# Rearranging the five planned instruction queues of a two-layer transformer kernel by a table

## The chip, the cores and the metric

The kernel runs on one core of a Trainium2 chip. The core has five engines, each with an instruction queue of its own that is worked through in order: TensorE (PE in the profile, with its weight loads shown as PEld), VectorE (DVE), ScalarE (ACT), GpSimd (POOL) and SyncE (SP, which here issues all the DMA transfers). Engines wait for each other by semaphores. The metric is the device time of one execution in microseconds; a kernel's time is the median of its runs.

## The reference

The sequence has S = 2048 rows of D = 448 values; there are 16 heads of 28, and the MLP is 1792 wide. The same two blocks run twice, which makes two layers:

```python
def _A_ref(x, wqkv, wo):
    ...
    scores = jnp.einsum("bhqd,bhkd->bhqk", q, k) * (Dh ** -0.5)
    p = _softmax(scores, axis=-1)
    o = jnp.einsum("bhqk,bhkd->bhqd", p, v)
    return (lambda x, *d: x.transpose(*d))(o, 0, 2, 1, 3).reshape(B, S, D) @ wo

def _B_ref(x, w1, w2, w3, w4):
    h = _gelu(_layernorm(x, axis=-1) @ w1)
    ...
    hs = jnp.concatenate([g0, g1, g2, g3], axis=-1) @ w2
    x1 = x + hs
    h2 = _gelu(_layernorm(x1, axis=-1) @ w3) @ w4
    return x1 + h2

x = A_x
x = x + _A_ref(_layernorm(x, axis=-1), A_wqkv, A_wo)
x = x + _B_ref(_layernorm(x, axis=-1), B_w1, B_w2, B_w3, B_w4)
x = x + _A_ref(_layernorm(x, axis=-1), A_wqkv, A_wo)
x = x + _B_ref(_layernorm(x, axis=-1), B_w1, B_w2, B_w3, B_w4)
```

In `_B_ref`, g0 to g3 are the four column groups of h, shifted along the sequence by 1 or 2 rows forward or back. All inputs are bf16.

## The kernel before

**Attention.** Keys and queries are held transposed, one head per 32 partitions. A score matmul (line L1544) multiplies 32 rows of keys with 512 (in places 256) queries and fills one PSUM bank. PSUM has eight banks. Scores fill banks 0 to 2 together (a unit of three banks) and then banks 3 and 4 (a unit of two), by turns; the two or three score matmuls of a unit are called its burst. ACT turns each unit into exponentials with one instruction (L1783), 386 of them of 128x1536 and 395 of 128x1024, and writes bf16 into the buffer PT. PT holds 15 banks' worth, so that the exponentials of a unit write where those of six units earlier stood, and must wait until these were read. The reader is the product with the values, PV (L1800): a group of four matmuls, each on its own 32 columns of the array, which adds into bank 5. A few blocks of scores go to bank 6 or 7 instead and get their exponentials on DVE by a chain of integer and float operations (L1626, L1653, L1655, L1657, L1660, output PD).

**The rest of the work.** Layer norms (statistics on DVE and POOL), the projections for keys, queries and values, the output projection and the MLP of one part of the sequence are woven into the attention of another. Their matmuls are groups of four on PE, mostly at L949, and write banks 6 and 7; DVE, and ACT at the end, take the results out. The gelu of the MLP (L2237) runs on ACT in large pieces with a load of ACT's function table before and after each; the gelu before w2 is made from tanh (L2056), in the table that the exponentials use. Where normalised rows must be transposed, PE does it at the very start and end (L1173, copied out by DVE at L1180), and elsewhere they go to DRAM and back by two DMAs, written in the profile as `xnd<-xn` and `xT<-xnd`. 1041 groups of filler matmuls (L2283), whose results nobody reads, stand in PE's queue as well.

**The head.** The first keys need the weights (L975 and L977 load them in pieces of 128 and of 64 rows), a repacking on ACT (L1078), squares on ACT (L1090) whose column sums PE makes (L940), the transposed input, the key projection (L949 with wk_pad), then a bias and the query, and the first burst.

**What sets the order.** The kernel is written as generators (one for scores, one for exponentials, one for PV, and so on) that yield operations. A planner, class `Sched`, runs them against a cost table, ranks and due times, and writes 9450 operations into a `Plan`, each in the queue of its engine. `Plan.finalize` turns the dependencies into semaphore waits, and `emit` writes each queue out. Between planning and `finalize` a plan can be rearranged: `Plan.rearranged(moves, weave)` takes each pair (a, b) out of `moves`, unlinks operation number a from its engine's queue and links it in behind b, an operation of the same engine. Then it merges the five queues again in the order that the letters of `weave` give (t, s, v, g, d for PE, ACT, DVE, POOL, SP), working out the dependencies anew, and insists that every operation reads what it read before. The core of it:

```python
for (a, b) in moves:
    p, q = prv[a], nxt[a]
    nxt[p] = q
...
for (a, b) in moves:
    q = nxt[b]
    nxt[b], prv[a], nxt[a] = a, b, q
...
for c in weave:
    k = "tsvgd".index(c)
    h = heads[k]
    eng, fn, reads, writes, deps, dma, t_end = self.args[h]
```

In the kernel before, both tables are empty (`MOVES = ()`, `WEAVE = ()`, lines 19 and 20), and the call (`if WEAVE: P = P.rearranged(MOVES, "".join(WEAVE))`, line 2339) isn't made: the planner's order stands.

Of the kernel before, what the change touches and what calls it, by code (L numbers as in the profile page):

```python
# [15 lines left out]
ENGS = ("pe", "act", "dve", "pool", "sp")  # L16


MOVES = ()
WEAVE = ()  # L20

FILL_MORE = ()

# [690 lines left out]
def build_kernel(nc, A_x, A_wqkv, A_wo, B_x, B_w1, B_w2, B_w3, B_w4, out, n_layers=2):  # L714
# [85 lines left out]
    with st:  # L800
# [1531 lines left out]
        def again(fn, k):  # L2332
            return lambda e: [x for _ in range(k) for x in fn(e)]

        for (i, k) in FILL_MORE:
            args = P.args[i]
            assert args[0] == "pe" and args[2] == [("ident",)]
            P.args[i] = (args[0], again(args[1], k)) + args[2:]
        if WEAVE:
            P = P.rearranged(MOVES, "".join(WEAVE))  # L2340
        P.finalize(nc, st)
# [55 lines left out]
```

## Time and profile before

| what | us |
|---|---|
| median of three runs | 1025.24 |
| the runs | 1026.08, 1025.24, 1024.41 |
| the profiled execution | 1024.58 |
| its span in the profile | 1022.9 |
| PE busy | 960.4 |
| ACT busy | 983.0 |
| DVE busy | 798.5 |
| POOL busy | 284.3 |
| first exponential starts | 15.89 |
| last exponential has ended by | 969.85 |

The span is what the trace covers; 1.7 us of the profiled execution's time lie around it. Busy times are sums of instruction durations in which overlaps count once. An exponential starts while the one before is still in flight, so that its duration is longer than the distance between the starts of two of them. A matmul's row with "x4" is one group on four parts of the array, which run side by side.

### The profile page before, as it was taken

The page shows a single profiled execution, that of the slowest core. Times are in us where ns is not written, and L with a number is a line of the kernel's source. Part 1 is how long each engine was busy: PE and PEld are TensorE (multiplying, and loading weights), DVE is VectorE, ACT ScalarE, POOL GpSimd, SP SyncE. Part 2 cuts the span into 40 slices and gives each one's busy share as a digit, 9 for nine tenths or more (in the row PEclk, how much of TensorE's full clock was granted, in tenths as well). Part 3 has the DMA queues.
Part 4 walks back from the last instruction along what each step waited for, and adds up shares of the span by engine and source line. Part 5 has one row for each costly group of instructions (what it writes and reads, how often), then busy time and mean ns, then how long its engine had stood idle before and what let it go on. Part 6 is the DMA issues. An engine that isn't in the chain of part 4 may idle for free.

```text
span 1022.9 us, 37404 instructions
## 1 busy us (share of the span) xinstructions
PE 960.4 (94%) x16925; PEld 399.8 (39%) x16925; DVE 798.5 (78%) x1557; ACT 983.0 (96%) x898; POOL 284.3 (28%) x453
## 2 busy tenths in 40 slices
PE   8999999999989999989999899999999999999998
PEld 3332444343322344333433334334333433344475
DVE  8778988899888858887887866788788578788751
ACT  8999999999999999999999999999999999999942
POOL 3212121520343015353453301221434120432130
PEclk9999999999999999999999999999999999999999
DMA  4443331321330014110122223522312020311000
GB/s 121 140 112 103 98 105 48 58 53 36 76 66 23 13 42 101 28 42 24 48 71 70 64 62 109 150 63 87 81 25 37 28 59 17 61 46 24 13 21 25
DMA packets 99399, 62.65 MB, mean 61 GB/s; under 512 B 68712, under 2 KB 88552, under 8 KB 99240
## 3 DMA queue, kind: packets, MB, share of 16 engines
q1 hardware_dynamic: 99240, 60.27, 23.4%
q8 instruction: 132, 2.16, 0.9%
q14 instruction: 27, 0.22, 0.1%
HBM read 28.16 MB, written 16.76 MB: 44 GB/s over the span
## 4 chain that ended last, share of the span: by engine, by line
ACT 90%; PE 7%; DVE 1%; DMA 1%; issue 0%; SPq 0%; DVEq 0%; ACTq 0%
ACT PT L1783 83%; PE ps L949 6%; ACT h2T L2237 2%; ACT fb L2056 2%; ACT L1783 1%; ACT L2237 1%; DMA xT<-xnd 1%; PE ps L1544 1%; ACT vaug L2237 1%; ACT kT L2237 1%; DMA xnd<-xn 0%; DMA PT<-in_A_wqkv_dram 0%; PE ps L1800 0%; ACT sq L1279 0%; PE ps L940 0%
## 5 line engine op out<-in xcount | busy, mean ns | idle before, releaser
L1783 ACT ACTIVATE PT<-ps 128x1024 bf16<-128x1024 f32 (+1 forms) x781 | 890.8, 1406 | 2.3 <-PE ps L1544 2.2
L1544 PE MATMUL ps<-qT,kT 32*128 32x512 bf16 (+1 forms) x2304 | 268.9, 335 | 39.3 <-ACT PT L1783 30.5
L1800 PE MATMUL ps<-PT,vaug 128*32 128x512 bf16 (+1 forms) x2432 | 200.1, 340 | 0.0
L1544 PEld LDWEIGHTS ps<-qT,kT 32*128 32x128 bf16 x2304 | 69.5, 91 | 276.3 <-ACT PT L1783 269.0
L949 PE MATMUL ps<-xT,w 128*32 128x512 bf16 (+4 forms) x2656 | 169.5, 345 | 1.4 <-DVE PD L1657 1.2
L2283 PE MATMUL ps<-ident 128*32 128x256 bf16 x4164 | 156.3, 276 | 1.5 <-POOL ident L1034 1.5
L2283 PEld LDWEIGHTS ps<-ident 128*32 128x32 bf16 x4164 | 105.2, 97 | 40.9 <-issue 21.3
L1626 DVE TENSOR_SCALAR yd<-ps 128x512 int32<-128x512 f32 x97 | 66.5, 686 | 34.2 <-PE ps L1544 33.2
L949 PEld LDWEIGHTS ps<-xT,w 128*32 128x32 bf16 (+1 forms) x2656 | 63.0, 95 | 62.7 <-issue 32.0
L1800 PEld LDWEIGHTS ps<-PT,vaug 128*32 128x32 bf16 x2432 | 62.9, 95 | 48.0 <-issue 38.0
L1655 DVE SCALAR_TENSOR_TENSOR fb<-fb,yd 128x512 f32<-128x512 f32 x97 | 69.2, 714 | 0.8
L1660 DVE SCALAR_TENSOR_TENSOR PD<-yd,PD 128x512 int16<-128x512 int16 x97 | 67.9, 700 | 1.0
L1653 DVE SCALAR_TENSOR_TENSOR fb<-yd 128x512 f32<-128x512 uint16 x97 | 67.8, 703 | 0.5
L949 PE MATMUL ps<-w,h2T 128*32 128x448 bf16 x1008 | 64.4, 355 | 0.7 <-ACT h2T L2237 0.7
L1897 POOL TENSOR_TENSOR otn<-ub,fb 128x512 bf16<-128x512 f32 (+1 forms) x23 | 26.5, 1154 | 136.8 <-DMA fb<-rscr 129.4
L2215 DVE CAST h2T<-ps 128x512 bf16<-128x512 f32 (+1 forms) x67 | 42.4, 633 | 13.4 <-PE ps L949 12.4
L1140 POOL TENSOR_SCALAR vpe<-mv 128x1 f32<-128x1 f32 (+2 forms) x21 | 8.3, 393 | 149.3 <-DVE mv L1135 149.3
L1282 POOL TENSOR_TENSOR sq<-qT 128x512 bf16<-128x512 bf16 x24 | 28.1, 1175 | 66.9 <-DVE qT L1341 65.6
L1282 POOL TENSOR_TENSOR sq<-kT 128x512 bf16<-128x512 bf16 (+2 forms) x32 | 31.6, 994 | 52.9 <-DVE kT L1296 42.8
L1544 PE MATMUL ps<-wk_pad,kT 32*128 32x512 bf16 x256 | 39.0, 384 | 7.3 <-ACT PT L1783 6.2
L1657 DVE TENSOR_SCALAR PD<-fb 128x512 bf16<-128x512 f32 x98 | 41.5, 424 | 1.0
L949 PE MATMUL ps<-xT,wq_pad 128*32 128x512 bf16 x512 | 39.3, 382 | 0.7 <-DVE vaug L1386 0.7
(195 smaller groups left out, 1243.5 us busy)
## 6 DMA issues: line engine op xcount, KB each, us to landing
uscr<-ub SPq DMA_DIRECT2D x28, 256.0 KB
ub<-uscr SPq DMA_DIRECT2D x28, 256.0 KB
fb<-rscr SPq DMA_DIRECT2D x24, 256.0 KB
xnd<-xn SPq DMA_DIRECT2D x28, 128.0 KB, 2.0
xd<-x_res SPq DMA_DIRECT2D x16, 224.0 KB, 3.1
x_res<-xd SPq DMA_DIRECT2D x16, 224.0 KB, 3.1
w<-in_B_w_dram SPq DMA_DIRECT2D x5, 448.0 KB, 8.4
obf<-in_A_x_dram SPq DMA_DIRECT2D x16, 112.0 KB, 2.1
```

The source lines that it names most:

```text
L949: r.append(e.matmul(out=out[c:c + w, :], lhsT=lhsT[:, c:c + w], rhs=rhs, start=start, stop=stop, tile_position=(0, c)))
L1282: return both("sq", 0.15 + NW * 0.0018, 0.07 + NW * 0.00104, lambda e: e.tensor_tensor(out=sq[:, si, 0:NW], in0=src, in1=src, op=ALU.mult) ...
L1544: yield op("pe", (0.005 + NW * 0.00042) / nc_, lambda e, i=i, kc=kc, j=j, g=g, qt=qt, a=a, NW=NW, bank=bank: e.matmul(out=ps[:, bank, i * ...
L1626: yield op("dve", c_ps(512), lambda e: e.tensor_scalar(out=y, in0=ps[:, bi(bank), :], scalar1=SCALE * L2E * FS, scalar2=-126.0 * FS, op0=A ...
L1653: yield op(D_[0][0], D_[0][1], lambda e: e.scalar_tensor_tensor(out=q, in0=lo, scalar=E2 / E3 * FS, in1=lo, op0=ALU.add, op1=ALU.mult), re ...
L1655: yield op(D_[1][0], D_[1][1], lambda e: e.scalar_tensor_tensor(out=q, in0=q, scalar=E1 / E3 * FS * FS, in1=lo, op0=ALU.add, op1=ALU.mult) ...
L1660: yield op(D_[3][0], D_[3][1], lambda e: e.scalar_tensor_tensor(out=pdt.bitcast(I16), in0=hi, scalar=128.0, in1=pdt.bitcast(I16), op0=ALU. ...
L1783: yield op("act", EXPC + n * w * 0.000833, lambda e, bk=bk, s0=s0, n=n, w=w: e.activation(out=PT[:, s0:s0 + n, 0:w], in_=ps[:, bk[0]:bk[0] ...
L1800: r.append(e.matmul(out=ps[32 * j:32 * j + 32, 5, 0:NW], lhsT=vaug[:, vs, 32 * (4 * g + j):32 * (4 * g + j) + 32], rhs=buf[:, s, i * NW:(i ...
L2215: ev = op("dve", c_ps(m * NW), lambda e, hr=hr, pv=pv: e.tensor_copy(out=hr, in_=pv), reads=[("ps", bi(b))], writes=hk, touch=[b])
L2237: yield op("act", c_act(len(fr_) * NW), lambda e, v=v: e.activation(out=v, in_=v, func=ACT.Gelu_apprx_tanh), reads=allk, writes=allk, tab= ...
L2283: return [e.matmul(out=ps[32 * c:32 * c + 32, bi(b), 0:256].rearrange("p (a n) -> p a n", n=128), lhsT=ident[:, 32 * c:32 * c + 32], rhs=i ...
```

## The change

Only the two tables are filled. `MOVES` has 3607 pairs and `WEAVE` 9450 letters, so the rearranging is now done. The planner, its own tables and all generators stay, and so do the number, the engine and the shape of every instruction. Lines below the tables stand 420 further down in the file: L1544 becomes L1964, L1783 becomes L2203, L1800 becomes L2220, L949 becomes L1369, L940 becomes L1360, L2283 becomes L2703.

```diff
-MOVES = ()
-WEAVE = ()
+MOVES = (
+    (109, 61), (110, 109), (111, 110), (112, 111), (113, 69), (114, 113), (74, 86), (71, 74), (75, 71), (70, 75), (73, 70), (72, 73), (98, 72),
...
```

By rank in its queue, most of PE's operations move (5196 of 6198, by 4.3 places on average), and nearly all of DVE's, POOL's and SP's (1395 of 1557, 426 of 449, 322 of 362; by 5 to 8 places). On ACT 143 of 884 move, none of the exponentials by more than two places and none of the large gelus. The sequence of the units stays. Three places on PE follow.

The first is the start of PE's queue, where the first key projection of layer 1 stands (L949 with wk_pad; `ones_bf` marks the column sums at L940, `ident,xn` the transposes). Before:

```order
2 L1173 MATMUL ps<-ident,xn 128x128 x8
3 L2283 MATMUL ps<-ident 32x256 x36
4 L1173 MATMUL ps<-ident,xn 128x128
5 L940 MATMUL ps<-ones_bf,PT 128x1 x4
6 L1173 MATMUL ps<-ident,xn 128x128 x7
7 L2283 MATMUL ps<-ident 32x256 x28
8 L940 MATMUL ps<-ones_bf,fb 128x1 x4
9 L949 MATMUL ps<-xT,wk_pad 32x512 x8
10 L940 MATMUL ps<-csum,astat 128x8
11 L949 MATMUL ps<-xT,wk_pad 32x512 x8
```

Now:

```order
2 L1593 MATMUL ps<-ident,xn 128x128 x12
3 L1360 MATMUL ps<-ones_bf,PT 128x1
4 L1593 MATMUL ps<-ident,xn 128x128 x3
5 L1360 MATMUL ps<-ones_bf,PT 128x1 x2
6 L1593 MATMUL ps<-ident,xn 128x128
7 L1360 MATMUL ps<-ones_bf,PT 128x1
8 L2703 MATMUL ps<-ident 32x256 x4
9 L1369 MATMUL ps<-xT,wk_pad 32x512 x12
10 L1360 MATMUL ps<-ones_bf,fb 128x1 x4
11 L1369 MATMUL ps<-xT,wk_pad 32x512 x4
```

The fillers that stood between the transposes have gone ahead of them, and 12 of the 16 matmuls of the key projection stand before the second column sums instead of behind them. On SP the piece of 64 rows of the key weights is now issued before the piece of 128.

The second place is PE's queue at the turn from layer 1 to layer 2 (402 us in the trace of before), around the first key projection of layer 2. Before:

```order
1081 L1800 MATMUL ps<-PT,vaug 32x256 x8
1082 L2283 MATMUL ps<-ident 32x256 x12
1083 L1544 MATMUL ps<-qT,kT 128x256 x4
1084 L949 MATMUL ps<-xT,wk_pad 32x512 x4
1085 L1800 MATMUL ps<-PT,vaug 32x256 x8
1086 L949 MATMUL ps<-xT,wk_pad 32x512 x8
1087 L1544 MATMUL ps<-qT,kT 128x256 x6
```

Now:

```order
948 L2220 MATMUL ps<-PT,vaug 32x256 x16
949 L1964 MATMUL ps<-qT,kT 128x256 x6
950 L2703 MATMUL ps<-ident 32x256 x28
951 L1369 MATMUL ps<-xT,wk_pad 32x512 x4
952 L1964 MATMUL ps<-qT,kT 128x256 x4
953 L1369 MATMUL ps<-xT,wk_pad 32x512 x8
954 L1964 MATMUL ps<-qT,kT 128x256 x6
955 L2220 MATMUL ps<-PT,vaug 32x256 x4
```

The projection's first group, which waits for `xT<-xnd`, stands ahead of the two-bank burst (here x4, of half width) instead of behind it, and the PV groups that stood behind the projection's first group have moved up or down a burst.

The third place is PE's queue in the second half (792 us in the trace of before), where the MLP's first matmuls (`xT,w`) run beside scores; x3 and x2 at the score line are the bursts, and x5 is two bursts in a row. Before:

```order
2219 L1544 MATMUL ps<-wk_pad,kT 128x512 x5
2220 L949 MATMUL ps<-xT,w 32x384 x4
2221 L1800 MATMUL ps<-PT,vaug 32x512 x4
2222 L949 MATMUL ps<-xT,w 32x384 x12
2223 L949 MATMUL ps<-xT,w 32x512 x3
2224 L949 MATMUL ps<-xT,w 16x512
2225 L1544 MATMUL ps<-wk_pad,kT 128x512 x3
2226 L1800 MATMUL ps<-PT,vaug 32x512 x4
2227 L949 MATMUL ps<-xT,w 32x384 x4
2228 L1544 MATMUL ps<-wk_pad,kT 128x512 x2
```

Now:

```order
1907 L1964 MATMUL ps<-wk_pad,kT 128x512 x3
1908 L1369 MATMUL ps<-xT,w 32x512 x3
1909 L1369 MATMUL ps<-xT,w 16x512
1910 L1369 MATMUL ps<-xT,w 32x384 x16
1911 L1964 MATMUL ps<-wk_pad,kT 128x512 x2
1912 L2220 MATMUL ps<-PT,vaug 32x512 x8
1913 L1964 MATMUL ps<-wk_pad,kT 128x512 x3
1914 L1369 MATMUL ps<-xT,w 32x384 x8
```

The six groups of four between the second burst of the x5 and the next three-bank burst have become two, both PV, and the work ahead of the two-bank burst has grown from none to five groups.

66 lines of the change are left out of this document (added), and 354 rows, old and new, of the table MOVES.

## The prediction

> **What bounds the kernel now.** I began with the page: the span, the engines' busy time, the clock, and the shares of the chain of waits.
>
> ```profile
> span 1022.9 us, 37404 instructions
> PE 960.4 (94%) x16925; PEld 399.8 (39%) x16925; DVE 798.5 (78%) x1557; ACT 983.0 (96%) x898; POOL 284.3 (28%) x453
> PEclk9999999999999999999999999999999999999999
> ACT 90%; PE 7%; DVE 1%; DMA 1%; issue 0%; SPq 0%; DVEq 0%; ACTq 0%
> ```
>
> ACT is busiest and owns nine tenths of the chain; PE, at 94%, is a close second, never throttled. The table by stretches (PE, PEld, DVE, ACT, POOL, clock) says where that changes:
>
> ```profile
> 32.00:64.00 32.00, 31.07 (x471) 11.08 (x471) 23.11 (x53) 32.00 (x30) 11.01 (x13) 1.00 0.59 158
> 384.00:416.00 32.00, 29.82 (x612) 13.13 (x608) 24.50 (x50) 30.79 (x29) 16.38 (x33) 1.00 0.38 82
> 864.00:896.00 32.00, 29.37 (x588) 12.87 (x580) 22.99 (x47) 31.30 (x26) 11.87 (x27) 1.00 0.29 53
> 992.00:1023.00 31.00, 27.95 (x648) 17.29 (x640) 7.19 (x14) 8.67 (x17) 4.50 (x6) 0.99 0.09 29
> ```
>
> So there are three stages. In the middle ACT has hardly a gap; at the end PE works and ACT idles; the head, before the first exponential, is a chain of single steps. The middle's limits are these rows:
>
> ```profile
> 15.89 2.38 ACT L1783 ACTIVATE PT<-ps 128x1536 bf16<-128x1536 f32 x2
> 969.85 1.28 ACT L2211 ACT_TABLE_LOAD   x1
> L1783 ACT ACTIVATE PT<-ps 128x1536 bf16<-128x1536 f32 x386 | 625.3, 1620 | 1.8 <-PE ps L1544 1.8
> L1783 ACT ACTIVATE PT<-ps 128x1024 bf16<-128x1024 f32 x395 | 470.5, 1197 | 0.5 <-PE ps L1544 0.4
> 206.43 1.34 ACT PT L1783
> 279.88 2.25 ACT PT L1783 x2
> 657.77 84.96 ACT PT L1783 x75
> ```
>
> The exponentials fill 15.9 to 969.9 us, 954 us. One is in flight while the next begins, so their durations (1620 and 1197 ns) overlap; the chain shows the pitch: 1.34 us for one of three banks, 2.25 for a pair, hence 0.91 for one of two. 386 x 1.34 + 395 x 0.91 is 877 us that no order can remove; the 84.96 us for 75 of them (1.133 each, against 2.25 / 2 = 1.125) shows a long stretch within 1% of that floor. Going through all starts on ACT and adding what each lies beyond the usual pitch of its shape gives **11.3 us of lateness** between 16 and 971 us: the whole prize in the middle. The waits agree:
>
> ```profile
> PEld ps L1544 <- ACT PT L1783: 312.2, 755, 1.2
> ACT PT L1783 <- PE ps L1544: 2.2, 4, 1.2
> ```
>
> Scores wait for ACT 755 times, 312.2 / 755 = 0.41 us each; ACT waits visibly for scores only 4 times. The rest of its lateness is hidden inside the durations of early-started instructions.
>
> **The change, the middle.** Nothing is removed or added: the same instructions on the same engines, so every gain is lateness and every loss new waiting. Where the lateness comes from shows in one place of PE's timeline:
>
> ```profile
> 792.06 0.39 PE L1544 MATMUL ps<-wk_pad,kT 32*128 32x512 bf16 x3
> 792.95 0.39 PE L1544 MATMUL ps<-wk_pad,kT 32*128 32x512 bf16 x2 [0.49 <-ACT PT L1783]
> 793.26 0.35 PE L949 MATMUL ps<-xT,w 128*32 128x384 bf16 x4
> 793.44 0.39 PE L1800 MATMUL ps<-PT,vaug 128*32 128x512 bf16 x4
> 793.65 0.88 PE L949 MATMUL ps<-xT,w 128*32 128x384 bf16 x16
> 794.46 0.39 PE L1544 MATMUL ps<-wk_pad,kT 32*128 32x512 bf16 x3
> 794.78 0.40 PE L1800 MATMUL ps<-PT,vaug 128*32 128x512 bf16 x4
> ```
>
> The burst of three must run while ACT does a two-bank exponential: 0.91 - 0.39 = 0.52 us of room. The burst of two has 1.34 - 0.39 = 0.95. Before, the tight burst has the more work ahead of it: 1.2 us (793.26 to 794.46) here. Over the whole PE order I count 5.63 groups of four other matmuls ahead of a three-bank burst and 2.90 ahead of a two-bank one; the change makes that 4.35 and 4.03. A group costs 22.70 / 128 = 0.18 us by the chain's last stretch:
>
> ```profile
> 997.28 22.70 PE ps L949 x512
> ```
>
> So the tight burst comes 1.28 x 0.18 = 0.23 us sooner on average, paid with 1.13 x 0.18 = 0.20 us from the burst with twice the room. Places with six or more groups of real work (no fillers) ahead of the tight burst fall from 57 to 37, and rise from 4 to 28 ahead of the other.
>
> What that buys, from the 11.3 us: the turn between the layers has the largest single gap, and table loads begin late seven times, about 0.35 us each, 2.5 together; I let both stay. Gaps of 0.27 to 0.62 us between exponentials and at 27.6 us, such as these, add up to 3.4:
>
> ```profile
> 427.27 3.71 ACT L1783 ACTIVATE PT<-ps 128x1536 bf16<-128x1536 f32 x3 [0.33 <-PE ps L1544]
> 887.42 1.02 ACT L1783 ACTIVATE PT<-ps 128x1024 bf16<-128x1024 f32 x1 [0.39 <-PE ps L1544]
> 888.70 3.71 ACT L1783 ACTIVATE PT<-ps 128x1536 bf16<-128x1536 f32 x3 [0.26 <-PE ps L1544]
> ```
>
> I take two thirds of those, 2.3 us, and half of the 3.7 us that is scattered in gaps under 0.2 us, 1.8: **-4.1 us**. The bounds: all of both and half the table gaps, -8; above, the losses priced under the rivals, +6.
>
> **The turn (402 us).** The largest gap of ACT, 1.21 us idle and 1.64 beyond pitch, hangs on two DMAs one after the other:
>
> ```profile
> 394.13 3.49 DMA xnd<-xn
> 397.68 5.84 DMA xT<-xnd
> 401.64 0.39 PE L1544 MATMUL ps<-qT,kT 32*128 32x256 bf16 x4
> 403.56 0.40 PE L949 MATMUL ps<-xT,wk_pad 128*32 128x512 bf16 x4 [1.53 <-DMA xT<-xnd]
> 404.99 5.97 ACT L1783 ACTIVATE PT<-ps 128x1536 bf16<-128x1536 f32 x5 [1.21 <-PE ps L1544]
> ```
>
> The first key projection of layer 2 waits 1.53 us on PE for its transposed input, and the burst for the next exponential is queued behind it. The change leaves these two transfers in the same sequence on SP and sets the projection one two-bank burst earlier. Then that burst, at 401.64 before, is behind the wait as well. If the data land at the same 403.5 us, exponential 323 is late in place of 324: it would start at 402.4 us and now at about 404.3, and the three-bank burst after it is no longer behind anything, so the loss is about the old 1.6 us plus 0 to 0.4. I take **0**, with -1.2 (data earlier, as PE and DVE around it run ahead) and +1 as bounds.
>
> **The head.** Before, the first key projection on PE stands behind column sums that wait for ACT, though DVE finished its input earlier:
>
> ```profile
> 8.72 0.25 PE L940 MATMUL ps<-ones_bf,PT 128*128 128x1 bf16 x4 [0.53 <-ACT PT L1090]
> 9.20 0.76 DVE L1180 COPY xT<-ps 128x512 bf16<-128x512 bf16 x2 [0.74 <-PE ps L1173]
> 10.19 0.25 PE L940 MATMUL ps<-ones_bf,fb 128*128 128x1 bf16 x4
> 10.37 0.62 PE L949 MATMUL ps<-xT,wk_pad 128*32 128x512 bf16 x8
> ```
>
> The input is there at 9.20 + 0.76 = 9.96, the projection starts at 10.37. With 12 projections ahead of the second column sums it can start at 9.96: 0.41 us saved at once. The transposes also lose most of the 0.53 us wait. Against that, SP now issues the small piece of the key weights first, about 0.5 us before the large one, which may land that much later. I take **-0.4 us**, bounds -1 and +0.5.
>
> **The tail.** Behind the last burst, PE has 1182 matmuls left instead of 1190: three projection groups fewer, one PV group more, 2 x 0.18 = **-0.4 us**, bounds -1 and +1, since nothing but PE's own work lies on the chain there.
>
> The sum is -4.1 + 0 - 0.4 - 0.4 = -4.9 us on the profiled execution: 1024.58 (its span and 1.7 us around it) becomes 1019.7. That execution lies 0.66 under the median of the three runs, 1025.24, so for a median I say **1020.0**, between 1019.7 and 1020.3.
>
> [...]
>
> **The rivals.**
>
> *PV releases the buffers late (slower).* An exponential writes buffers that PV of six exponentials earlier must have read. Before, that PV stands behind the exponential's own burst on PE in 4 cases; in the new order in 34, and in 173 instead of 10 only one burst lies between. PV costs about 0.22 us (793.44 to 793.65). After a tight burst only 0.52 us of room less any lateness is left, so each of the 34 costs 0 to 0.4 us, and where the PE is already behind, some of the 173 cost 0.1. With 0.25 x 34 = 8.5 the sum becomes +3.6: **1028**. It decides above 0.15 us a place (4.9 / 34). For it: PE is 94% busy, so there is little to catch up with. Against: 24 of the 34 are two-bank exponentials, whose bursts have 0.95 us of room, and the mean wait of 0.41 us says PE is usually ahead.
>
> *The lateness stays (no change).* If the gaps are set by DVE and DMA, as PE's stalls at the turn and at 886 us are, then bursts moved past other work still stand behind the same waits. Head and tail give 0.8, the middle nothing: **1024**. For it: the biggest gap is a DMA's. Against: the scattered gaps all fall on the exponential behind the two-bank one, which is the mark of the tight burst.
>
> [...]
>
> *More is gained.* The table gaps and the turn close too: 2.5 + 1.2 on top: **1016**.
>
> **How the numbers follow.** Forecast 0.53, late PV 0.18, nothing moved 0.15, clock 0.05, more 0.09. A measurement here tells about 0.2% (2 us) from no change. Forecast and "more" are faster except for a tail of the forecast within 2 us (0.02): 0.60; no change 0.15 and that tail: 0.17; slower 0.23. The likeliest case's own range is 1016.5 to 1023; to hold 8 in 10 it must reach to the late-PV case and half of "more": **1014.5 to 1028.5**.
>
> **What would show it.** Right: ACT's idle and hidden lateness between 16 and 971 us falls from 11.3 to about 7; the rows at 427 and 887 lose their releaser PE ps; the first exponential starts near 15.5; scores' mean wait for ACT stays near 0.4 us; from the last burst to the end about 54 us as before. Late PV would show as ACT PT L1783 waiting for PE ps at the PV line, and as pairs longer than 2.25. [...] I am wrong if ACT's lateness grows, or if the turn's gap becomes several us because other transfers on SP's reordered queue land later.

## The result, and the profile after

The change made the kernel **slower**: 1032.12 us against 1024.93 us (medians of six runs each), a ratio of 1.0072 with an interval of 1.0059 to 1.0085. The profiled execution took 1031.42 us, its span 1029.5: 6.8 and 6.6 more than before. A gain of 4.9 us was forecast.

The same parts of the page as before the change (span, busy time, the chain by engine), of the changed kernel:

```profile
span 1029.5 us, 37441 instructions
PE 963.0 (94%) x16922; PEld 409.8 (40%) x16925; DVE 796.9 (77%) x1557; ACT 983.6 (96%) x898; POOL 274.0 (27%) x453
ACT 73%; PE 13%; DVE 8%; POOL 3%; DMA 1%; issue 1%; SPq 0%; DVEq 0%
```

PE, DVE and ACT are as busy as they were, within 3 us. But the chain that ended last runs over ACT for 73% of the span in place of 90%: PE, DVE and POOL have taken the rest. Work that used to be hidden under the exponentials now sets their time in places. Going through all starts on ACT as in the prediction gives 17.3 us of lateness between 16 and 971 us, in place of 11.3.

The two rows of waits that stood in the prediction, and two that show what is new (what waited, for whom, us in all, times, longest):

```profile
PEld ps L1964 <- ACT PT L2203: 243.4, 583, 1.1
ACT PT L2203 <- PE ps L1964: 5.4, 9, 1.7
PEld ps L2703 <- DVE yd L2046: 5.2, 14, 0.8
PE ps L1369 <- POOL sq L1702: 0.9, 2, 0.7
```

Scores had to wait for ACT to free their banks 172 times less often than before: this harmless wait, in which PE is ahead of ACT, fell from 312.2 to 243.4 us. Waits of PE and its weight loads for DVE, summed over all rows of the view, rose from 50.0 us in 160 times to 68.7 in 225, and those for POOL from 3.2 to 10.1. (The two queues of PE overlap, so these are not 19 us of time; they say how often a group came to PE before its bank or its input was there.) The third row is one of the new kinds: fillers, which nobody needs, wait for DVE to empty the bank that they would write, and the burst stands behind them.

Where the time went shows best by the starts of the same exponentials in the two profiled executions, after minus before. This is worked out from ACT's rows, 781 in each:

| exponential | start before, us | later after, us | what lies in between |
|---|---|---|---|
| 0 | 15.9 | 0.8 | head |
| 100 | 130.8 | 0.3 | some given back |
| 120 | 153.2 | 1.3 | a stall at 137 us |
| 240 | 300.0 | 2.9 | small ones at 193 to 232, and 298 us |
| 420 | 526.5 | 3.0 | the turn is as late as before |
| 440 | 551.7 | 3.6 | 543 us |
| 520 | 650.5 | 3.5 | |
| 540 | 673.3 | 5.8 | 676 us |
| 780 | 968.6 | 6.1 | |
| end of PE | 1019.95 | 6.6 | tail |

So there is no slow drift; there are some eight places.

The same rows also tell what ACT waited for. In the changed kernel 14 exponentials start 0.2 us or more beyond the usual pitch behind another one, 9.0 us together. Each of the 14 starts 0.04 to 0.08 us after a score matmul ends; of the 663 that are on time 55 do. So in each of these places the burst came last, and not a PV that had to free the buffer. In the 3 us ahead of ten of the 14, PE or its weight loads had waited 0.3 us or more for DVE (eight) or for a square on POOL (two, at 298 and 300 us); of the 663 that are on time this holds for 85. Of the other four one is the turn, with its transfer, and one follows on the stall at 676 us; at 415 us the view names nothing, and at 104 us only ACT.

**The largest** begins on DVE. Three views of the changed kernel from 672 us on: DVE and POOL first.

```profile
672.75 0.74 DVE L2293 SCALAR_TENSOR_TENSOR ub<-ub,fct,ps 128x512 f32<-128x512 f32 x1
673.41 1.13 DVE L1986 TENSOR_SCALAR qT<-qT,db 128x512 bf16<-128x512 bf16 x1
674.46 0.67 DVE L1790 TENSOR_TENSOR wk_pad<-wk_pad,ps 128x512 bf16<-128x512 bf16 x1
673.35 1.04 POOL L1702 TENSOR_TENSOR sq<-wk_pad 128x512 bf16<-128x512 bf16 x1 [2.78 <-PE ps L1369]
L1986 DVE TENSOR_SCALAR qT<-qT,db 128x512 bf16<-128x512 bf16 x28 | 11.3, 404 | 0.2
```

The operation at 674.46 empties a bank. In the planner's order the query shift at 673.41 stood 19 places ahead of it on DVE; the change put the shift, and another correction like the one at 674.46, close ahead of it. It also took 1130 ns where its kind takes 404 (347 where no POOL operation runs beside it); a POOL operation ran from 673.35 to 674.39. Then PE, ACT and the stretches of 2 us (PE, PEld, DVE, ACT, POOL, clock):

```profile
673.88 0.39 PE L1964 MATMUL ps<-qT,kT 32*128 32x512 bf16 x3 [0.63 <-ACT PT L2203]
675.28 1.90 PE L1369 MATMUL ps<-xT,wq_pad 128*32 128x512 bf16 x16 [1.01 <-DVE wk_pad L1790]
677.11 0.61 PE L1964 MATMUL ps<-qT,kT 32*128 32x512 bf16 x2
677.76 1.02 ACT L2203 ACTIVATE PT<-ps 128x1024 bf16<-128x1024 f32 x1 [1.68 <-PE ps L1964]
672.00:674.00 2.00, 1.37 (x20) 0.37 (x17) 2.00 (x4) 2.00 (x3) 0.65 (x1) 1.00 0.00 0
674.00:676.00 2.00, 0.99 (x11) 0.34 (x12) 1.13 (x2) 2.00 (x2) 0.39 (x1) 0.79 0.47 169
676.00:678.00 2.00, 2.00 (x18) 0.42 (x14) 0.78 (x2) 0.32 (x2) 0.00 (x0) 0.50 0.68 197
678.00:680.00 2.00, 2.00 (x33) 0.69 (x29) 1.09 (x3) 1.72 (x2) 1.08 (x1) 0.85 0.07 11
```

The query projection waits 1.01 us for that bank with the burst of unit 539 behind it. PE had little work just before (1.37 and 0.99 us of 2 busy), and the granted clock went to 0.50: the same 16 matmuls take 1.90 us, against 1.05 for a projection of 16 at full clock. ACT stands idle for 1.68 us.

**The stall at 137 us** has the same shape; here a PV group waits for the sum in bank 5:

```profile
133.66 1.83 POOL L2317 TENSOR_TENSOR otn<-ub,fb 128x512 bf16<-128x512 f32 x1 [11.11 <-DMA fb<-rscr]
134.28 1.76 DVE L2080 SCALAR_TENSOR_TENSOR PD<-yd,PD 128x512 int16<-128x512 int16 x1
135.96 0.73 DVE L2293 SCALAR_TENSOR_TENSOR ub<-ub,fct,ps 128x512 f32<-128x512 f32 x1
136.75 0.61 PE L2220 MATMUL ps<-PT,vaug 128*32 128x512 bf16 x8 [1.07 <-DVE ub L2293]
137.73 4.76 ACT L2203 ACTIVATE PT<-ps 128x1024 bf16<-128x1024 f32 x4 [0.57 <-PE ps L1964]
```

**The head**, on PE and ACT:

```profile
2.72 5.22 PE L2703 MATMUL ps<-ident 128*32 128x256 bf16 x124 [2.72 <-POOL ident L1454]
9.99 0.83 PE L1369 MATMUL ps<-xT,wk_pad 128*32 128x512 bf16 x12 [0.74 <-DVE xT L1600]
12.45 1.82 ACT L1483 ACTIVATE vaug<-ones_bf 128x368 bf16<-128x368 bf16 x1
16.66 2.36 ACT L2203 ACTIVATE PT<-ps 128x1536 bf16<-128x1536 f32 x2
```

The first key projection starts at 9.99, near the forecast (9.96); the run of the fill below shows that other executions start it later. But a fill of 1.82 us, which stood in ACT's idle time at 3.5 us, now stands behind the first key copy, ahead of the squares and the first query copy. The first exponential comes at 16.66 in place of 15.89.

One thing must be known to read what follows. A program here runs at one of a few mean granted clocks, and its time goes with it. Of 85 runs of the kernel before, taken beside the experiments, 44 had 1.000 and averaged 1024.4 us, 25 had 0.998 (1025.9), 13 had 0.997 (1027.5) and 3 had 0.995 (1028.6). Of the six runs of the changed kernel one had 1.000 (1031.0), three 0.998 (1031.9) and two 0.995 (1033.9). So **6.6 us are lost at the full clock**, by one run of the changed kernel; at 0.998 it is 6.0 and at 0.995 it is 5.2. Five of six runs fell below 1.000, against 41 of 85 before; six are few. Where an experiment has runs at 1.000 their mean is given beside the ratio. It is over few runs, and the mean of the kernel before at 1.000 itself lies between 1023.8 and 1024.9 us from one experiment's set of runs to the next, so that differences under 1 us say little.

### The profile page after: what moved, and what is told of

Its sections match the earlier page's. It is cut to its first block, busy times and chain, and to the rows that moved or that the text cites. A ratio compares the mean times of both kernels' runs of the same rounds, so it can differ in the third digit from the quotient of the medians.

```text
span 1029.5 us, 37441 instructions
## 1 busy us (share of the span) xinstructions
PE 963.0 (94%) x16922; PEld 409.8 (40%) x16925; DVE 796.9 (77%) x1557; ACT 983.6 (96%) x898; POOL 274.0 (27%) x453
## 4 chain that ended last, share of the span: by engine, by line
ACT 73%; PE 13%; DVE 8%; POOL 3%; DMA 1%; issue 1%; SPq 0%; DVEq 0%
ACT PT L2203 68%; PE ps L1369 8%; PE ps L1964 2%; ACT h2T L2657 2%; PE ps L2703 2%; ACT fb L2476 1%; PE ps L2220 1%; DVE st L1554 1%; ACT L2203 1%; ACT L2657 1%; DVE PD L2080 1%; POOL sq L1702 1%; DMA xT<-xnd 1%; DVE yd L2046 1%; DVE PD L2077 1%
## 5 line engine op out<-in xcount | busy, mean ns | idle before, releaser
L2203 ACT ACTIVATE PT<-ps 128x1024 bf16<-128x1024 f32 (+1 forms) x781 | 890.7, 1360 | 5.9 <-PE ps L1964 5.4
L1964 PE MATMUL ps<-qT,kT 32*128 32x512 bf16 (+1 forms) x2304 | 277.9, 335 | 37.6 <-ACT PT L2203 30.6
L2220 PE MATMUL ps<-PT,vaug 128*32 128x512 bf16 (+1 forms) x2432 | 179.1, 341 | 1.6 <-DVE ub L2293 1.1
L1964 PEld LDWEIGHTS ps<-qT,kT 32*128 32x128 bf16 x2304 | 73.1, 91 | 265.8 <-ACT PT L2203 212.2
L1369 PE MATMUL ps<-xT,w 128*32 128x512 bf16 (+4 forms) x2656 | 154.4, 344 | 3.5 <-DMA xT<-xn 1.2
L2703 PE MATMUL ps<-ident 128*32 128x256 bf16 x4164 | 153.1, 276 | 4.6 <-POOL ident L1454 2.7
L2703 PEld LDWEIGHTS ps<-ident 128*32 128x32 bf16 x4164 | 100.2, 97 | 48.9 <-issue 24.2
L1369 PEld LDWEIGHTS ps<-xT,w 128*32 128x32 bf16 (+1 forms) x2656 | 59.6, 95 | 61.5 <-issue 22.8
L2220 PEld LDWEIGHTS ps<-PT,vaug 128*32 128x32 bf16 x2432 | 55.4, 95 | 63.5 <-issue 41.5
L1369 PE MATMUL ps<-w,h2T 128*32 128x448 bf16 x1008 | 60.0, 354 | 0.3 <-ACT h2T L2657 0.3
L1964 PE MATMUL ps<-wk_pad,kT 32*128 32x512 bf16 x256 | 40.3, 384 | 5.1 <-ACT PT L2203 4.6
L1560 POOL TENSOR_SCALAR vpe<-mv 128x1 f32<-128x1 f32 (+2 forms) x21 | 5.9, 286 | 135.9 <-DVE mv L1555 135.6
L1369 PE MATMUL ps<-xT,wq_pad 128*32 128x512 bf16 x512 | 36.9, 389 | 2.4 <-ACT sq L1699 1.4
```

The source lines that it names most:

```text
L1369: r.append(e.matmul(out=out[c:c + w, :], lhsT=lhsT[:, c:c + w], rhs=rhs, start=start, stop=stop, tile_position=(0, c)))
L1964: yield op("pe", (0.005 + NW * 0.00042) / nc_, lambda e, i=i, kc=kc, j=j, g=g, qt=qt, a=a, NW=NW, bank=bank: e.matmul(out=ps[:, bank, i * ...
L2203: yield op("act", EXPC + n * w * 0.000833, lambda e, bk=bk, s0=s0, n=n, w=w: e.activation(out=PT[:, s0:s0 + n, 0:w], in_=ps[:, bk[0]:bk[0] ...
L2220: r.append(e.matmul(out=ps[32 * j:32 * j + 32, 5, 0:NW], lhsT=vaug[:, vs, 32 * (4 * g + j):32 * (4 * g + j) + 32], rhs=buf[:, s, i * NW:(i ...
L2703: return [e.matmul(out=ps[32 * c:32 * c + 32, bi(b), 0:256].rearrange("p (a n) -> p a n", n=128), lhsT=ident[:, 32 * c:32 * c + 32], rhs=i ...
```

## The experiments

Eighteen kernels were run. Where a diff shows rows, they are rows of an engine's queue, in the line numbers of the kernel before, as in all profiles of experiments.

### Undoing single pieces

**One fill put back on ACT.** Two pairs of the table give way to one:

```diff
-(47, 7), (21, 137)
+(47, 21)
```

> The changed kernel with one operation of ACT put back: the 1.82 us fill of vaug with ones (L1063) stands behind the other fill at the start again, not behind the first key copy. Theory 'the head lost on ACT': the query copy and the first exponential come 1.2 us sooner (15.4 us in place of 16.7) and the whole follows, 1031.0 (-0.8 to -1.4 against 1032.1). Rival 'the head is refunded later': the first exponential comes sooner, the end does not, 1032.

1032.26 us, 1.0066 (1.0048 to 1.0084). The first exponential came 0.3 us sooner, not 1.2. PE's and ACT's rows of this kernel:

```profile
2.73 6.06 PE L2283 MATMUL ps<-ident 128*32 128x256 bf16 x124 [2.73 <-POOL ident L1034]
10.83 0.83 PE L949 MATMUL ps<-xT,wk_pad 128*32 128x512 bf16 x12 [0.74 <-DVE cols L1026]
16.35 2.36 ACT L1783 ACTIVATE PT<-ps 128x1536 bf16<-128x1536 f32 x2
```

From the start of the key projection to the first exponential it takes 5.52 us here, as it does in the kernel before (10.37 to 15.89). In the changed kernel it takes 6.67 us, and 6.67 to 6.69 in the six other traces that have the fill behind the key copy. So **the fill costs 1.15 us**, as expected. What hid it is the start of the projection, 10.83 in place of 9.99, because the transposes wait behind 124 fillers, which took 6.06 us in place of 5.22. The last section shows why these take longer in one execution than in another; in five other traces with the same fillers ahead the projection starts at 10.12 to 10.77. The clock dropped at 138 us (a mean of 0.95 from 128 to 160 us). Inconclusive on the total.

**The whole head back.** The 174 operations ahead of the first exponential stand as before in all five queues; on PE:

```diff
-L2283 MATMUL ps<-ident 32x256 x124
-L1173 MATMUL ps<-ident,xn 128x128 x12
+L2283 MATMUL ps<-ident 32x256 x64
+L1173 MATMUL ps<-ident,xn 128x128 x8
+L2283 MATMUL ps<-ident 32x256 x36
```

> The changed kernel, but the 174 operations planned ahead of the first exponential stand in all five queues as before the change. Theory 'the head lost 0.8 us to fillers ahead of the transposes and to the fill on ACT': the first exponential at 15.9 again in place of 16.7, 1031.3 (-0.5 to -1.1). Rival: the gain is lost by 100 us, 1032.

1033.41 us, 1.0082 (1.0063 to 1.0102); one run at full clock, 1031.2. The first exponential came 1.1 us sooner than in the changed kernel (0.3 ahead of before). The end did not follow: the clock dropped in two places, at 408 and at 678 us (means of 0.95 from 384 to 416 us and of 0.89 from 672 to 704 us), and the exponentials fell behind there by 1.2 and 3.2 us. The head's own 0.8 us is there in the trace and not to be seen in the total.

**Two late releases on DVE put first**, those of the two stalls above:

```diff
-L1655 SCALAR_TENSOR_TENSOR fb<-fb,yd 128x512
-L1660 SCALAR_TENSOR_TENSOR PD<-yd,PD 128x512
-L1873 SCALAR_TENSOR_TENSOR ub<-ub,fct,ps 128x512
+L1873 SCALAR_TENSOR_TENSOR ub<-ub,fct,ps 128x512
+L1655 SCALAR_TENSOR_TENSOR fb<-fb,yd 128x512
+L1660 SCALAR_TENSOR_TENSOR PD<-yd,PD 128x512
...
-L1370 TENSOR_TENSOR wk_pad<-wk_pad,ps 128x512
-L1873 SCALAR_TENSOR_TENSOR ub<-ub,fct,ps 128x512
-L1566 TENSOR_SCALAR qT<-qT,db 128x512
-L1370 TENSOR_TENSOR wk_pad<-wk_pad,ps 128x512
+L1370 TENSOR_TENSOR wk_pad<-wk_pad,ps 128x512 x2
+L1873 SCALAR_TENSOR_TENSOR ub<-ub,fct,ps 128x512
+L1566 TENSOR_SCALAR qT<-qT,db 128x512
```

> The changed kernel with two operations of DVE moved: the one that frees bank 6 at 674 us (L1370) stands ahead of a query shift (L1566) and of another correction, and the one that frees bank 5 at 136 us (L1873) ahead of a shift, a copy and an exponential step. Theory 'DVE frees banks late because less urgent operations now stand ahead': PE's waits at 137 and 675 us vanish, the clock does not drop at 676, 1029 to 1031 (-1 to -3). Rival 'DVE is late as a whole': the waits stay within 0.3 us of their size, 1032.

1031.61 us, 1.0067 (1.0054 to 1.0080). ACT's and PE's rows of this kernel at the second place:

```profile
671.57 15.08 ACT L1783 ACTIVATE PT<-ps 128x1536 bf16<-128x1536 f32 x13
675.73 1.05 PE L949 MATMUL ps<-xT,wq_pad 128*32 128x512 bf16 x16
```

Thirteen exponentials without a gap, the projection without a wait and at full clock: in this trace the stall at 676 us is gone, its drop of the clock included, so it **was the late release on DVE**. At 137 us the wait moved on: fillers now waited there and exponential 106 was 0.75 us late in place of 105 by 0.87. The total gained nothing: three of four runs had the full clock and averaged 1031.3. Nor does this trace end sooner. The 2.2 us that the place cost between exponentials 520 and 540 are gone, but 1.1 us were lost between 300 and 340, around the turn, where the changed kernel lost 0.2, and 1.3 between 540 and 640, where it lost 0.2. The price of the place itself depends on the clock: in the run with the new order in the second half alone, below, the projection waits the same 1.01 us, the clock holds, and the place costs 0.8 us.

**All 28 query shifts put back** near their old places on DVE (the change had set them 27 places later on average; 8 are left):

```diff
-L1386 CAST vaug<-ps 128x16x28
 L1566 TENSOR_SCALAR qT<-qT,db 128x512
+L1386 CAST vaug<-ps 128x16x28
...
```

> The changed kernel with the 28 query shifts on DVE (L1566), which the change set 27 places later on average, put back; all else as changed. Theory 'less urgent DVE operations now stand ahead of releases': 1029 to 1030.5, the gaps at 137 and 678 us gone. Rival 'the shifts are only two of many': 1031.5 to 1032.5.

1031.77 us, 1.0052 (1.0034 to 1.0071); the one run at full clock took 1031.8. The interval overlaps that of the changed kernel. The gap at 678 us was smaller, others stood: the rival fits better.

### Bursts put ahead of what PE waited at

**Eight bursts in the changed kernel**; one of the eight places:

```diff
 L949 MATMUL ps<-xT,wq_pad 32x512 x4
-L1800 MATMUL ps<-PT,vaug 32x512 x8
-L1544 MATMUL ps<-qT,kT 128x512 x2
+L1544 MATMUL ps<-qT,kT 128x512 x2
+L1800 MATMUL ps<-PT,vaug 32x512 x8
...
```

> The changed kernel with eight bursts (units 105, 236, 237, 330, 539, 552, 706, 737) put ahead of the group that PE was waiting at in front of them. Theory 'stalls ahead of bursts': the gaps of ACT at 138, 298, 300, 415, 678, 693, 888 and 924 us shrink by some 4 us in all, and the granted clock's drop at 676 us does not come; 1028. Rival 'the stall only moves on' (the next burst is late in place of this one): 1031 to 1032.

1031.19 us, 1.0062 (1.0038 to 1.0085); 1030.0 at full clock (two runs), 1.1 less than the one such run of the changed kernel. Lateness 15.7 us in place of 17.3. At 678, 693 and 888 us the gaps shrank to 0.4 us or less and the clock held. At 138, 300 and 415 us the gap came back one or two units later: 1.05 us at unit 106, 0.33 at 238, 0.59 at 331.

**All repairs together**: the head as before, the two releases, and fourteen bursts.

```diff
-L2283 MATMUL ps<-ident 32x256 x124
+L2283 MATMUL ps<-ident 32x256 x64
...
```

> The changed kernel with the head as before, the two operations of DVE of the previous run moved, and fourteen bursts put ahead of the groups that PE waited at. If the losses are separate and local, they add up: 1032.1 - 0.8 (head) - 2 (the drop and its stall) - 3 (other places) = 1026 to 1027.5. Rival 'the order is late as a whole, and a repaired place only passes it on': 1030 or more.

1031.25 us, 1.0063 (1.0050 to 1.0076), 1030.3 at full clock. Some 5 us were expected. New gaps had come at 300 and 303 us (0.95 and 1.01), 418 (1.36) and 852 (0.64). The first three lie just behind repaired places: what was repaired there was passed on.

**Eight bursts in the kernel before**, at its own gaps:

```diff
-L1544 MATMUL ps<-qT,kT 128x256 x4
+L1544 MATMUL ps<-qT,kT 128x256 x10
 L949 MATMUL ps<-xT,wk_pad 32x512 x4
 L1800 MATMUL ps<-PT,vaug 32x256 x8
-L949 MATMUL ps<-xT,wk_pad 32x512 x8
-L1544 MATMUL ps<-qT,kT 128x256 x6
...
```

> The kernel before, with eight bursts (units 86, 270, 324, 342, 528, 711, 712, 744) put ahead of the groups that PE waited at or worked through in front of them, 21 operations of PE moved; all other queues as before. Theory 'stalls ahead of bursts': ACT's lateness falls from 11.3 by about 3 us (the gaps at 405, 427 and 887 us above all), the time to 1021 to 1022.5. Rival 'the stall only moves on': 1024 to 1026, with new gaps behind the old places.

1025.36 us against 1025.10, 1.0006 (0.9994 to 1.0017); 1024.7 at full clock, where the runs of before beside it have 1024.2. No gain. The turn shows why (PE and ACT of this kernel):

```profile
403.82 0.39 PE L1544 MATMUL ps<-qT,kT 32*128 32x256 bf16 x6 [0.88 <-ACT PT L1783]
404.66 0.40 PE L949 MATMUL ps<-xT,wk_pad 128*32 128x512 bf16 x4 [0.45 <-DMA xT<-xnd]
411.32 0.40 PE L949 MATMUL ps<-xT,w 128*32 128x512 bf16 x4 [1.60 <-issue]
406.50 1.02 ACT L1783 ACTIVATE PT<-ps 128x1024 bf16<-128x1024 f32 x1 [0.48 <-PE ps L1544]
412.30 1.02 ACT L1783 ACTIVATE PT<-ps 128x1024 bf16<-128x1024 f32 x1 [0.78 <-PE ps L1544]
```

The moved burst (403.82) is no longer behind the transfer. But the projection still starts when its data are there, 404.66, and the work that waited for it stands ahead of the next bursts: exponential 325 is 0.9 us late in place of 324 by 1.6, and PE waits 1.60 us at 411, for what the view does not name, ahead of a group that it ran without a wait before. Here a late input moved lateness along the queue; **to move one burst ahead of it did not make it less late**.

### Taking the order apart

**PE's projections and MLP groups back** between the bursts where they stood before, all else as changed (a piece of PE's queue):

```diff
-L1544 MATMUL ps<-qT,kT 128x512 x3
-L949 MATMUL ps<-sq,astat 32x512 x4
-L949 MATMUL ps<-wv,xT 32x448 x16
 L949 MATMUL ps<-sq,astat 32x512 x4
 L1544 MATMUL ps<-qT,kT 128x512 x5
...
```

> The changed kernel, but on PE every group that is neither score, PV nor filler stands between the same two bursts as before the change; all other queues as changed. Theory 'stalls ahead of bursts' (groups that wait for DVE, POOL or a DMA were moved ahead of a burst, which then waits with them): ACT's lateness between 16 and 971 us falls from 17.3 to about 12, the time to 1027 to 1028. Rival 'PV releases late': nothing moves, 1032 within 1.

1108.33 us, 1.0807 (1.0777 to 1.0836). **PV back** in the same way:

```diff
-L1544 MATMUL ps<-qT,kT 128x512 x5
-L1800 MATMUL ps<-PT,vaug 32x512 x4
+L1544 MATMUL ps<-qT,kT 128x512 x2
+L1800 MATMUL ps<-PT,vaug 32x512 x4
+L1544 MATMUL ps<-qT,kT 128x512 x3
...
```

> The changed kernel, but on PE every PV group stands between the same two bursts as before the change. Theory 'stalls ahead of bursts': 1032 within 1, ACT's lateness stays at 16 to 18. Rival 'PV releases late': -4 to -6, 1027.

1058.33 us, 1.0322 (1.0286 to 1.0357). **By engine**: PE and ACT in the new order, the other three near the old; and the reverse. Both are made by merging the queues anew, so the edit is the table as a whole (2738 and 1016 pairs in place of 3607):

```diff
-MOVES = (
-    (109, 61), (110, 109), (111, 110), (112, 111), (113, 69), (114, 113), (74, 86), (71, 74), (75, 71), (70, 75), (73, 70), (72, 73), (98, 72),
...
```

> The order of the changed kernel on PE and ACT; DVE, POOL and SP as near the order before as the data allow. Theory 'PE's order loses the time by itself': 1030 to 1034. Theory 'the queues only fit each other' (PE waits for releases that the other queues have later or sooner): well above the changed kernel, 1040 to 1060, as when only PV or only the groups were put back. Theory 'DVE's late releases lose it': 1024 to 1027.

> The order before on PE and ACT; DVE, POOL and SP as near the order of the change as the data allow. Theory 'DVE's late releases lose it': 1030 to 1034. Theory 'PE's order loses it': 1024 to 1026. Theory 'the queues only fit each other': 1040 or more.

1269.57 us (1.2382, 1.2346 to 1.2418) and 1312.58 us (1.2817, 1.2777 to 1.2857). In the first PE waits like this:

```profile
PE ps L949 <- POOL otn L1897: 33.7, 4, 11.8
PE ps L1800 <- DVE ub L1873: 22.3, 6, 10.6
```

Both of my theories for the two class runs failed: each part taken alone costs five to forty times what the change does. **The queues only fit each other**: in a mixed order the releases on DVE and POOL come up to 11.8 us after PE has reached the group that needs them. These four runs so cannot say which class of moves lost the 7 us, and PV's part is not isolated by them. What speaks against late PV is the trace: no row of ACT waiting for PE's PV line is in the changed kernel's view of waits, and the 14 late exponentials all follow a burst.

**By stretch of time**: the new order up to exponential 240 and the old from there; and the old, then the new. Each queue is cut at the same set of operations.

```diff
-MOVES = (
-    (109, 61), (110, 109), (111, 110), (112, 111), (113, 69), (114, 113), (74, 86), (71, 74), (75, 71), (70, 75), (73, 70), (72, 73), (98, 72),
...
```

> The order of the change up to the exponential of unit 240 (300 us), the order before from there on. Theory 'separate losses at fixed places': the head's 0.8, those at 137, 193 to 232 and part of that at 298 us, so 1027 to 1028.5, and the second half runs as before. Rival 'one loss carried by the whole order': 1025 to 1026 or, where the seam does not fit, well above 1032.

> The order before up to the exponential of unit 240, that of the change from there on. Theory 'separate losses at fixed places': the turn, 544, 678, 900 us and 0.5 at the tail, so 1028 to 1029.5; with the run before the two losses add up to 7 within 1.5. Rival 'one loss carried by the whole order': they do not add up.

1.0031 (1.0019 to 1.0044) and 1.0040 (1.0026 to 1.0055): the two losses add up to 0.0071, and the whole change has 0.0072. At full clock it is 1028.2 (three runs) and 1027.2 (two): 3.7 and 2.7 over 1024.44, together 6.4 or 6.5 against 6.6. The seam does no harm. In the profile of the second, all exponentials up to 240 start within 0.15 us of where they did before. So **the loss falls into two parts that add up, and more than half of it lies in the first 300 us**; there is no loss that the order as a whole carries. That the places within a part are just as separate is not shown: there a repair was passed on. In the second part the stall of the largest place stands as it did, without the drop of the clock:

```profile
672.35 1.05 PE L949 MATMUL ps<-xT,wq_pad 128*32 128x512 bf16 x16 [1.01 <-DVE wk_pad L1370]
670.00:672.00 2.00, 0.71 (x7) 0.12 (x7) 2.00 (x3) 2.00 (x3) 1.04 (x1) 1.00 0.02 3
672.00:674.00 2.00, 1.65 (x26) 0.60 (x26) 0.76 (x2) 1.39 (x2) 0.00 (x0) 1.00 0.95 288
```

### POOL beside DVE, and PE's lead

**Squares of 64 columns** in place of 512, in both kernels; seven eighths of the squares are left out, and POOL's other operations stay:

```diff
-lambda e: e.tensor_tensor(out=sq[:, si, 0:NW], in0=src, in1=src, op=ALU.mult)
+lambda e: e.tensor_tensor(out=sq[:, si, 0:64], in0=src[:, 0:64], in1=src[:, 0:64], op=ALU.mult)
```

> The kernel before, with the squares of L1282 (on POOL, some on DVE) over 64 of 512 columns; seven eighths of these squares are left out, and the norms made from them are wrong. Theory 'DVE stretched by POOL' (DVE's instructions last up to 1 us longer when a POOL operation runs beside them, and in the new order the stretched ones stand ahead of releases): the kernel before gains little, 1022 to 1025.

> The changed kernel with the same cut of the squares. Theory 'DVE stretched by POOL': the difference to the kernel before with the same cut shrinks from 7 us to 2 to 4. Theory 'the queues are late as a whole': it stays at 6 to 8.

1025.51 (1.0008, 0.9996 to 1.0021) and 1029.62 (1.0057, 1.0039 to 1.0075). By medians the difference is 4.1 us; at full clock 1023.7 (four runs) and 1029.4 (three), 5.7 in place of 6.6. In the profile of the second the stalls at 298 us (PE waiting for a square) and at 676 are gone, the others stand. So POOL's squares account for about 1 us of the loss, with 5.7 over seven runs against 6.6 over one run of the changed kernel, and they are not the main cause. POOL's other operations, among them the one beside the stall at 137 us, were not tested.

**Shorter fillers**, 192 columns in place of 256, in both kernels:

```diff
-bi(b), 0:256].rearrange("p (a n) -> p a n", n=128)
-rhs=ident[:, :].unsqueeze(1).to_broadcast([128, 2, 128])
+bi(b), 0:192].rearrange("p (a n) -> p a n", n=96)
+rhs=ident[:, 0:96].unsqueeze(1).to_broadcast([128, 2, 96])
```

> The kernel before with every filler matmul over 192 columns in place of 256; a quarter of the fillers' work, which nobody reads, is left out: PE has some 39 us less to do (a quarter of 156.3). Theory 'PE's lead is short': before gains little, 1022 to 1025, since its lead is 0.41 us a burst. If the clock drops, the time rises and the clock column shows it.

> The changed kernel with the same shorter fillers. Theory 'PE's lead is short': the difference to the kernel before with short fillers falls from 7 to 3.5 or less, 1026 to 1028. Rival 'late releases on DVE': the difference stays at 5 to 8, 1029 to 1032.

The kernel before became slower, 1028.47 (1.0025, 1.0014 to 1.0037), the changed one 1031.43 (1.0058, 1.0039 to 1.0078). The difference of the medians shrank to 3.0 us, but not for the theory's reason: no run of either had the full clock. Two stretches of the kernel before with short fillers:

```profile
160.00:192.00 32.00, 28.70 (x492) 11.59 (x488) 26.72 (x49) 30.96 (x29) 11.97 (x25) 0.89 0.33 55
864.00:896.00 32.00, 27.75 (x542) 11.84 (x534) 22.57 (x46) 29.31 (x23) 8.78 (x27) 0.95 0.31 51
```

Where the clocks are equal the comparison is cleaner, over one to five runs each: at 0.993 it is 1029.1 and 1034.2, so 5.1; at 0.995, 1027.7 and 1032.0, so 4.3; at 0.997, 1026.7 and 1030.9, so 4.2. With full fillers it is 5.2 at 0.995 (1033.9 less 1028.6). So PE's lead is worth 1 us at most by these few runs; whether it is worth anything stays open.

**Longer fillers**, 288 columns, in the kernel before:

```diff
-bi(b), 0:256].rearrange("p (a n) -> p a n", n=128)
+bi(b), 0:288].rearrange("p (a n) -> p a n", n=96)
```

> The kernel before with every filler matmul over 288 columns in place of 256 (results that nobody reads); PE has some 20 us more to do (an eighth of 156.3). Theory 'thin PE work loses the clock': of the runs far more than the 38 of 69 of the kernel before hold a mean clock of 1.000, and the median falls by 0.3 to 1 us in spite of the longer PE work, 1024 to 1025. Rival 'PE's lead is what counts': the clock does not change and the bursts come later, 1026 to 1029.

1027.14 us, 1.0010 (0.9999 to 1.0022). Seven of twelve runs held 1.000, of the runs of before on the same chip 6 of 16: too few to tell. At full clock it took 1026.8 against 1024.9 there: 1.9 us for some 20 us more of PE's filler work. The rival is nearer. No version that does the whole work beats the kernel before.

## Why the prediction was wrong

- **"What that buys" in the middle, -4.1 us, is the step that failed.** The count behind it may stand: bursts of three have less work ahead of them. But the step took the moved groups for work that is ready when it comes to PE. They are not: waits for DVE rose from 160 to 225 times and those for POOL from 3.2 to 10.1 us, and ahead of ten of the 14 late bursts PE had waited 0.3 us or more for one of the two. ACT's lateness rose by 6.0 us where a fall of 4.1 was forecast. The number of waits alone is no measure of the loss: the kernel with the new order from 300 us on has 216 waits for DVE and loses 2.7 us. The order had to be read on DVE too, for the distance from each release to the group that needs it; I read it on PE alone.
- That lateness can be taken away gap by gap was wrong in itself. Eight bursts put first in the kernel before removed named gaps and gave back nothing (1.0006). Gaps that I counted as a prize are the ends of late inputs. Of the two places named as signs, the gap at 427 us went and the one at 887 us stayed (0.6 us beyond pitch).
- **The head, -0.4, came out at +0.8.** The projection started at 9.99 where 9.96 was forecast, but that was luck: with the same order on PE it starts at 10.12 to 10.83 in six other traces, and with the old head at 10.11 to 11.05 in six. So little was gained at that step. What was missed is an instruction that the change moves on ACT, 1.82 us long, into the chain behind that start (1.15 us), and the fillers that went ahead of the transposes.
- The turn, taken at 0: right. The gap went from exponential 324 to 323 and from 1.64 to 1.59 us beyond pitch, as worked out there.
- The table loads, let stay: right, 0.29 to 0.41 us each.
- The tail, -0.4, came out at +0.5: from the start of the last exponential to the end of PE's work 51.3 us became 51.9. It is the order's own: four traces with the new tail have 51.8 or 51.9 and four with the old 51.3. Two groups fewer stand there in all, so some wait was added; which one was not looked into.
- **Of the rivals**, late PV had the right sign, half the size and the wrong mechanism: PV stands in the stalls as one that waits for DVE (137 us), not as one that ACT waits for. For the 0.05 given to the clock, and for its share in the +6 that bounds the middle, no run shows a source: they were the author's estimate. The runs showed this in its place: in the changed kernel the granted clock fell to 0.50 from 675.2 to 678.6 us, after thin work on PE (0.71 us busy of the 2 from 672.93 us), and by the runs sorted by clock one step of the mean clock goes with 1.1 to 1.6 us. That PE is "never throttled" was not so: the last row of the prediction's own table has 0.99, and PE's first fillers run at half pace (last section). "The lateness stays" named the true agent, DVE and DMA, and stopped at no change: that the same agent could make things worse was not priced.
- The range ended at 1028.5, 3.6 us short. The losses that were priced came one at a time; eight small ones of 0.3 to 2.2 us make it.

What stands as shown: the two parts of the loss add up, the stall at 676 us is a late release on DVE, the fill on ACT costs 1.15 us in the head, and by the trace the late exponentials wait for their bursts and not for PV. What was only read in the traces: that the other places are the same kind of stall. Open: why repairs within a part are passed on and win so little of the total, PE's share of lost lead, POOL's operations other than the squares, and the tail.

## What to carry to other kernels

An order that is written out by hand must be judged on all queues at once: for each group ask not only what stands ahead of it on its own engine, but how long before it the release that it needs comes on the other, and which urgent instruction has had a less urgent one put ahead of it. In this kernel, whose engines are 77 to 96% busy, a gap on the bound engine was the end of some late input; find that input, since moving the victim ahead only made the next one late. And take two orders apart by stretches of time, where the parts added up, rather than by engine, where they didn't fit.

## What the hardware showed

- **DVE instructions stretch beside POOL.** The exponential step at 134.28 us took 1760 ns (its kind 700, and 683 where no POOL operation runs beside it), while a POOL multiplication ran from 133.66 to 135.49; the shift at 673.41 took 1130 (its kind 404, and 347 where no POOL operation runs beside it) beside a square that ended at 674.39. The first ended 0.55 us after POOL's, the second 0.15. In the changed kernel's trace 25 of DVE's instructions last over 0.3 us more than the median of their kind, in that of the kernel before 23, and each of them has a POOL operation beside it. Most that have one don't stretch so far: they are 468 and 507 in all. Over a whole execution the longer ones of DVE's instructions take 20 us more than the medians of their kinds in the kernel before and 22 in the changed one: it is where the stretching falls that differs.
- **PE's first work runs at half pace, for a time that differs.** In the changed kernel's trace a group of four fillers follows the one before by 0.213 us up to 6.1 us and by 0.109 from there on; in the run of the fill the change comes at 7.8 us. The trace's own record of the granted clock begins to show 1.000 at 6.16 and 7.88 us. Up to there the record is empty, and the column of the stretches shows 1.00. In all seven traces with 124 fillers of 256 columns ahead of the transposes, the later that record begins (6.16 to 7.88), the later the first key projection starts (9.99 to 10.83).
- **The clock fell after thin work, without a long pause, and did not each time.** Ahead of the drop at 676 us PE's longest waits were 0.63 and 1.01 us, and from 672 us on it was busy for 1.64 of 3.17 us; by the trace's record the granted clock was then 0.50 from 675.17 to 678.58 us. With the new order in the second half alone PE waited for the same 1.01 us, and the clock held at 1.00, with the same work before it: the projection starts at 672.35 there and at 675.28 in the changed kernel, and in the 2 us from 670.00 there, as in those from 672.93 here, PE was busy for 0.71 with 7 matmuls. With fillers of 192 columns none of ten runs of the kernel before had 1.000, of the runs beside it 6 of 13. What makes the clock fall was not shown.
- **Runs sort by their mean clock** though nothing differs in the program: 1024.4, 1025.9, 1027.5 and 1028.6 us at 1.000, 0.998, 0.997 and 0.995. In the traces one spell of half clock of 3.4 us makes 0.998 (the changed kernel), and one of 3.4 and one of 6.8 us make 0.995 (the whole head back). A change of under 2 us has to be read among runs of equal clock.
